# A delta-rule attention and two MoE layers on one core: the order of the first two solve groups rewritten

## The chip, the core and the metric

One core of a Trainium2 chip runs the whole program in one launch. Its engines are TensorE (PE, with its weight loads shown apart as PEld), VectorE (DVE), ScalarE (ACT), GpSimd (POOL) and SyncE (SP, which issues most DMAs). Each engine works through its own instructions in the order in which they were written and waits on semaphores for the others. The metric is device microseconds of one launch, as the median of several runs.

## The reference, cut to what matters

```python
def _attn_ref(q, k, v, beta):            # B=4, H=8, S=768, D=48
    k_n = k / (np.linalg.norm(k, axis=-1, keepdims=True) + 1e-06)
    for t in range(S):
        y[:, :, t] = np.einsum('bhd,bhde->bhe', q[:, :, t], state)
        v_old = np.einsum('bhde,bhd->bhe', state, kt)
        state = state + bt[:, :, :, None] * np.einsum('bhd,bhe->bhde', kt, vt - v_old)

def _moe_ref(x, w_gate, w1, w2):         # N=3072, 384 wide, 8 experts of 1024
    P = sinkhorn(exp(x @ w_gate - max))  # 8 rounds
    for e in range(E):
        out += P[:, e:e + 1] * (np.maximum(x @ w1[e], 0.0) @ w2[e])

def _moe2_ref(x, w_in, w_out):           # 384 -> 2048 -> 384
    h = x @ w_in
    return (h / (1 + exp(-1.702 * h))) @ w_out
```

The three run one after the other: the output of the attention, 3072 rows of 384, is the input of the first MoE layer, whose output is the input of the second. Only the attention has a step-by-step recurrence.

## The kernel before, in words

**Units and groups.** The 768 steps are cut into pieces of 64 tokens. Two batches are worked on at once, so there are 24 units (`NU`), numbered u. A unit's 64 steps are done together: a triangular system of 64 by 64 per head is solved ahead of time, and the state S goes from unit to unit only through four small matrix products. Four units make a group (`NG` = 6 groups, g), and the triangular solve is done for a whole group at once.

**The chain of a unit** (`chain`, L357 to L416) has four steps s. Step 0: `ks` on PE (keys times state, L373), then `r` on DVE (`ks` minus the values, L375), and two ACT copies of S into `su`. For the first unit there is no state, and `r` is the negated values, by ACT (L379). Step 1: `up` on PE (the inverse times `r`, L384) and two ACT copies into `su` (L385, L386). Step 2: `sp` on PE (L395) and the new S, by DVE (L401) or, for unit 0, ACT (L399). Step 3: `y` on PE (L408) and a copy `ys` by ACT (L410).

**The solve of a group** (`prep`, L209 to L355) is a generator. It makes norms, weights (`wt`), masks (`bm`, L168) and scores (`pg` on PE, L182), masks the scores into `am` (L188), copies two strips of `am` (L266), transposes them into `ln` (L269), and runs a loop of 30 dependent steps on DVE (jj, L275 to L299, two operations each, `lt` then `ln`) that inverts the 32 by 32 diagonal blocks. Then `ln` is transposed twice, into `ta` (L314) and `tt` (L340), and the off-diagonal quarter is filled by `pz` and `px` on PE (L323, L332), each with two ACT copies after it. `up` of a unit needs its 8 of the group's 32 blocks of `tt` finished.

**Two generators interleaved.** The main loop walks through units and steps, t = 4u + s. After each step of the chain, `slot(t)` advances `prep` by so many pieces as a table says (`FIRST[t]` for t up to 15, `PIECES` after that). A jj step is worth one piece. From t = 10 (`LAG`) on, slots also put in pieces of expert 0 of the first MoE layer: logits `pl`, then `ph` and `po` (matrix products in three passes, L499 to L501). So expert 0 can first run when units 0 and 1 are done and their output `xb` is split, and from there it fills PE. The work of engines is thus ordered at build time: this code decides only in which order each engine sees its instructions.

**Weights of expert 0.** `split0` advances a generator that writes the low parts of the weights (`w1s`, `w2s`, L545), four DVE subtractions at each of four calls. Before, two calls lie in the head of group 1 and two in its loop, at jj 4 and 10.

After the attention the kernel runs the remaining seven experts and the second layer, in which PE is filled. The change doesn't touch that part.

Of the kernel before, what the change touches and what calls it, by code (L numbers as in the profile page):

```python
# [9 lines left out]
F32 = mybir.dt.float32  # L10
# [11 lines left out]
H = 8  # L22
D = 48
# [5 lines left out]
PIECES = (4, 2, 2, 1, 2, 4, 4, 4, 4, 4, 4, 4, 3, 3, 2, 2)  # L29
ITEMS = (6, 5, 5, 5, 5, 5, 5, 5, 5, 5, 5, 6, 5, 5, 5, 5)  # L30

FIRST = (0, 4, 3, 2, 2, 2, 2, 3, 3, 4, 5, 5, 5, 4, 4, 4)


LAG = 10
# [5 lines left out]
class Attention:  # L41
# [167 lines left out]
    def prep(self, g):  # L209

        nc, am, tt = self.nc, self.am, self.tt
        w, u = 2 * g, 4 * g
        if g == 0:
            self.square(0, nc.vector)
            self.square(1, nc.vector)
            self.norm(0)
            self.norm(1)
            self.weigh(0, 1)
            self.mask(0, eng=nc.vector)
            for v in range(1, 4):  # L220
                self.mask(v)
            for v in range(4):
                self.gram(v, (0,), 0, H, (self.psc, "c") if v < 2 else None)
            self.scale_v(0)
            self.scale_k(0)
            self.square(2)
            self.square(3)
            self.at = {(0, 13): lambda: [self.gram(v, (1,), 0, H) for v in range(4, 8)],
                       (0, 20): lambda: self.kept.update({v: self.gram(v, (0,), 0, H, self.early[v - 4])
                                                          for v in range(4, 8)}),  # L230
                       (0, 23): lambda: self.split0(), (1, 4): lambda: self.split0(), (1, 10): lambda: self.split0()}
            yield 1.0
        elif g == 1:
            self.weigh(2, 3)
            nc.gpsimd.tensor_copy(out=self.gate, in_=self.w[3][:, 1, 7:8])
            self.scale_k(1)
            self.mask_m(2)
            self.mask_m(3)
            yield 1.0
            for v in range(4, 8):  # L240
                self.mask(v, eng=nc.vector)
                self.kept[v]()
                if v % 2:
                    self.split0()
                yield 1.0
        else:
            for i in range(8):
                if i == 5:
                    self.mask(u + 3)
                self.gram(u + i // 2, (0, 1), i % 2 * 4, 4)  # L250
                if i == 1:
                    self.square(w + 1)
                elif i == 2:
                    self.norm(w + 1)
                elif i == 3:
                    self.weigh(w + 1)
                    self.mask(u + 2)
                elif i == 7:
                    self.scale_k(w)
                    self.scale_k(w + 1)  # L260
                yield 1.0

        ln = self.one.tile([128, 32, 32], F32, tag="ln", name="ln")

        for q in (32, 96):
            (nc.vector.tensor_copy if g == 0 and q == 32 else nc.scalar.copy)(  # L266
                out=am[q:q + 32, :, 0:32], in_=am[q:q + 32, :, 32:64])
            yield 1.0
        nc.vector.transpose(out=ln, in_=am[:, :, 0:32].rearrange("p m t -> p t m"))  # L269
        if g == 0:  # L270
            for v in range(4):
                self.gram(v, (1,), 0, H)
        yield 1.0
        nc.vector.memset(ln.rearrange("p t s -> p (t s)")[:, 0:1024:33], 1.0)
        for jj in range(1, 31):  # L275
            tmp = self.one.tile([128, 256], F32, tag="lt", name="lt")
            nr = 31 - jj
            t3 = tmp[:, 0:nr * jj].rearrange("p (a c) -> p a c", c=jj)
            nc.vector.tensor_tensor(  # L279
                out=t3, in0=ln[:, jj + 1:32, jj:jj + 1].to_broadcast([128, nr, jj]),  # L280
                in1=ln[:, jj:jj + 1, 0:jj].to_broadcast([128, nr, jj]), op=ALU.mult)
            yield 0.5
            nc.vector.tensor_tensor(out=ln[:, jj + 1:32, 0:jj], in0=ln[:, jj + 1:32, 0:jj], in1=t3, op=ALU.add)  # L283
            if (g, jj) in self.at:
                self.at[g, jj]()
            if 0 < g < NG - 1:
                if jj == 17:
                    self.square(w + 2)
                elif jj == 21:
                    self.norm(w + 2)  # L290

            if jj == 22 and 0 < g < NG - 1:
                step = self.weights(w + 2)
            elif jj > 22 and 0 < g < NG - 1:
                next(step, None)
            if jj == 30 and 1 < g < NG - 1:
                self.mask(u + 4)
                self.mask(u + 5)
            yield 0.5  # L299
        if g < 2:  # L300
            nc.gpsimd.tensor_copy(out=self.gate, in_=ln[:, 31, 29:30])
            if g == 0:
                self.mask_m(0)
                self.mask_m(1)
            else:
                self.scale_k(2)
                for v in range(4, 8):
                    self.mask_m(v)
                    if v == 5:
                        self.scale_k(3)  # L310
                self.mask(8)
                self.mask(9)
        ta = self.one.tile([128, 32, 32], F32, tag="ta", name="ta")
        nc.vector.transpose(out=ta.rearrange("p m s -> p s m"), in_=ln.rearrange("p t s -> p s t"))  # L314
        yield 1.0

        zs = ta

        def pz(m0, n):
            ps = self.psg.tile([128, n, 32], F32, tag="g", name="pz")  # L320
            for m in range(n):
                for q in (0, 64):
                    nc.tensor.matmul(ps[q + 32:q + 64, m], am[q:q + 32, m0 + m, 32:64],  # L323
                                     ta[q:q + 32, m0 + m], start=True, stop=True, tile_position=(q, q + 32))
            for q in (0, 64):
                nc.scalar.copy(out=zs[q + 32:q + 64, m0:m0 + n], in_=ps[q + 32:q + 64])

        def px(m0, n):
            ps = self.psg.tile([128, n, 32], F32, tag="g", name="px")
            for m in range(n):  # L330
                for q in (0, 64):
                    nc.tensor.matmul(ps[q:q + 32, m], zs[q + 32:q + 64, m0 + m],  # L332
                                     tt[q + 32:q + 64, m0 + m, 32:64], start=True, stop=True,
                                     tile_position=(q + 32, q))
            for q in (0, 64):
                nc.scalar.copy(out=tt[q:q + 32, m0:m0 + n, 32:64], in_=ps[q:q + 32])

        def tr(q, m0=0, n=32):
            if q is None:
                nc.vector.transpose(out=tt[:, :, 32:64].rearrange("p m t -> p t m"), in_=ln)  # L340
            else:
                nc.scalar.copy(out=tt[q:q + 32, m0:m0 + n, 0:32], in_=tt[q:q + 32, m0:m0 + n, 32:64])

        for f, *i in (((pz, 0, 16), (tr, None), (pz, 16, 16), (tr, 0), (tr, 64), (px, 0, 16), (px, 16, 16)) if g else
                      ((pz, 0, 8), (tr, None), (tr, 0, 0, 8), (tr, 64, 0, 8), (px, 0, 8), (tr, 0, 8, 24),
                       (tr, 64, 8, 24), (pz, 8, 8), (px, 8, 8), (pz, 16, 16), (px, 16, 16))):
            while f == tr and self.upped < u - 1:
                yield 1.0
            f(*i)
            if f == px and i[0] == 0:  # L350
                self.ready = g
                if g == 0:
                    self.norm(2)
                    self.norm(3)
            yield 1.0  # L355

    def chain(self, u):  # L357

        nc = self.nc
# [3 lines left out]
        x, tt, bk = self.X[w % 4], self.tt, self.bk[w % 4]  # L363
        tk = [slice(64, 128), slice(0, 64)]
        S = self.S
        r = self.wk.tile([128, H, D], F32, tag="r", name="r", bufs=1)

        su = self.wk.tile([128, 2, H, D], F32, tag="su", name="su", bufs=1)
        if not first:
            ks = self.psc.tile([128, H, D], F32, tag="c", name="ks")  # L370
            for h in range(H):
                for b in range(2):
                    nc.tensor.matmul(ks[tk[b], h], x[64 * b:64 * b + D, 0, j, h], S[64 * b:64 * b + D, h],  # L373
                                     start=True, stop=True)
            nc.vector.tensor_tensor(out=r, in0=ks, in1=self.V[w][:, j], op=ALU.subtract)  # L375
            nc.scalar.copy(out=su[0:64, 0], in_=S[0:64])
            nc.scalar.copy(out=su[64:64 + D, 1], in_=S[64:64 + D])
        else:
            nc.scalar.mul(r, self.V[w][:, j], -1.0)  # L379
        yield  # L380
        up = self.psc.tile([128, H, D], F32, tag="c", name="up")
# [79 lines left out]
def kernel(  # L461
# [281 lines left out]
    def slot(t):  # L743

        n, k = rate * ITEMS[t % 16] if t >= LAG else 0, (PIECES if t > 15 else FIRST)[t % 16]
        if t == LAG:
# [447 lines left out]
```

## Time and profile before

| | |
|---|---|
| median of 3 runs | 2224.41 us (2222.56 to 2230.47) |
| the profiled execution | 2232.75 us, its span 2230.4 us |
| PE, DVE, ACT, POOL busy in the span | 97%, 68%, 48%, 49% |
| first `pl` of expert 0 | 89.43 us after the start |
| first `pz` of group 1 | 115.00 us |
| mean granted TensorE clock | 0.975 of full speed |

A row of the timeline gives the start in us, the length in us, the engine, line, operation and tiles; in square brackets the idle time of the engine just ahead of it and what ended that. A row with x2 or x4 covers so many instructions in a line, and its length runs from the start of the first to the end of the last. PEclk is the clock that was granted to TensorE, as a share of full speed.

### The profile page before, as it was taken

Reading aid. Unit: us, or ns where it says so; the run is one execution under the profiler, and the core shown is the slowest. Engines: PE = TensorE matmul, PEld = TensorE weight load, DVE = VectorE, ACT = ScalarE, POOL = GpSimd, SP = SyncE. Lnnn points to the kernel's source line nnn. Section 1 sums busy time; section 2 is a strip of 40 time slices with the busy share of each in tenths; the row PEclk is TensorE's granted clock in tenths of the full one; section 3 lists DMA queues with packets and bytes.
Section 4 is the critical chain, followed back from the end, with each engine's and each line's share of the span. In section 5 each row is a group of like instructions: output and inputs, shape, how many; then the busy total and the mean of one; then the engine's idle time right before and its main releaser. Section 6 shows DMA issues by size and latency. Waiting matters only on the chain.

```text
span 2230.4 us, 40903 instructions
## 1 busy us (share of the span) xinstructions
PE 2156.8 (97%) x15663; PEld 1953.7 (88%) x15663; DVE 1526.7 (68%) x2792; ACT 1068.0 (48%) x2126; POOL 1096.8 (49%) x1275
## 2 busy tenths in 40 slices
PE   5799999998999999999999999999999999999999
PEld 4778888896989999999999999999999989889998
DVE  7847775627777777767776777777775556776676
ACT  4334434434444544444445444455544446565554
POOL 4141123224776776666552656556665434662333
PEclk8689999998999999999999999999999999999999
DMA  6223333348335343333448655565554465567231
GB/s 159 51 62 81 105 100 102 90 127 294 136 115 184 124 168 136 115 144 110 159 164 275 185 178 182 170 200 178 188 199 143 136 239 164 172 192 246 92 121 50
DMA packets 229154, 336.74 MB, mean 151 GB/s; under 512 B 15648, under 2 KB 192416, under 8 KB 224800
## 3 DMA queue, kind: packets, MB, share of 16 engines
q1 hardware_dynamic: 228096, 332.86, 46.1%
q8 instruction: 123, 2.02, 0.4%
q10 hardware_dynamic: 864, 1.28, 0.2%
q14 instruction: 71, 0.58, 0.1%
HBM read 204.58 MB, written 129.50 MB: 150 GB/s over the span
## 4 chain that ended last, share of the span: by engine, by line
PE 85%; DVE 9%; DMA 2%; POOL 1%; ACT 1%; issue 1%; SPq 0%; POOLq 0%; ACTq 0%; DVEq 0%
PE po L501 14%; PE po L499 14%; PE po L500 14%; PE c L500 11%; PE c L501 11%; PE c L499 11%; DVE lt L279 3%; DVE ln L283 3%; PE ph L499 1%; PE pg L182 1%; PE ph L500 1%; PE ph L501 1%; PE y L408 1%; PE sp L395 1%; PE px L332 1%
## 5 line engine op out<-in xcount | busy, mean ns | idle before, releaser
L501 PE MATMUL po<-w2c,h 128*128 128x384 f32 x1728 | 586.6, 339 | 1.4 <-DVE h L1007 1.3
L500 PE MATMUL po<-w2c,h 128*128 128x384 f32 x1728 | 587.3, 340 | 0.0
L499 PE MATMUL po<-w2c,h 128*128 128x384 f32 x1728 | 578.5, 335 | 1.1 <-ACT h L1005 1.1
L1062 POOL TENSOR_TENSOR acc<-acc,ye 128x384 f32<-128x384 f32 x252 | 261.6, 1038 | 381.7 <-ACT ye L1061 329.6
L501 PE MATMUL c<-xt,w1c 128*128 128x512 f32 x1080 | 429.1, 397 | 2.0 <-POOL w1c L496 2.0
L499 PE MATMUL c<-xt,w1c 128*128 128x512 f32 x1080 | 424.5, 393 | 4.4 <-DVE f L1039 2.3
L500 PE MATMUL c<-xt,w1c 128*128 128x512 f32 x1080 | 428.0, 396 | 0.0
L1039 DVE TENSOR_TENSOR o<-o,c 128x512 f32<-128x512 f32 x288 | 197.5, 686 | 246.7 <-PE c L501 231.5
L1064 DVE SCALAR_TENSOR_TENSOR acc<-po,P,acc 128x384 f32<-128x384 f32 x420 | 258.2, 615 | 150.6 <-PE po L501 150.3
L499 PEld LDWEIGHTS po<-w2c,h 128*128 128x128 f32 x1728 | 324.9, 188 | 41.0 <-ACT h L1005 1.7
L500 PEld LDWEIGHTS po<-w2c,h 128*128 128x128 f32 x1728 | 323.8, 187 | 40.1
L501 PEld LDWEIGHTS po<-w2c,h 128*128 128x128 f32 x1728 | 325.0, 188 | 4.3 <-DVE h L1007 4.3
L1061 ACT ACTIVATE ye<-po,P 128x384 f32<-128x384 f32 x252 | 146.6, 582 | 372.1 <-PE po L501 359.3
L501 PEld LDWEIGHTS c<-xt,w1c 128*128 128x128 f32 x1080 | 202.3, 187 | 47.0 <-POOL w1c L496 2.8
L996 ACT ACTIVATE h<-f 128x512 fp32r<-128x512 f32 x224 | 133.9, 598 | 192.8 <-DVE f L1039 191.0
L499 PEld LDWEIGHTS c<-xt,w1c 128*128 128x128 f32 x1080 | 203.0, 188 | 18.8 <-DVE f L1039 3.1
L1039 DVE TENSOR_TENSOR f<-o,c 128x512 f32<-128x512 f32 x288 | 199.2, 692 | 20.7 <-PE c L501 3.6
L500 PEld LDWEIGHTS c<-xt,w1c 128*128 128x128 f32 x1080 | 203.0, 188 | 9.8
L1032 ACT COPY o<-c 128x512 f32<-128x512 f32 x288 | 163.6, 590 | 59.7 <-PE c L501 58.2
L496 POOL TENSOR_TENSOR w2c<-w2r,w2c 128x384 fp32r<-128x384 f32 x140 | 149.4, 1067 | 47.7 <-ACT w2c L495 47.4
L1074 POOL TENSOR_TENSOR acc<-acc,ye 128x384 f32<-128x384 f32 x84 | 92.7, 1104 | 156.6 <-ACT ye L1073 154.0
L998 DVE SCALAR_TENSOR_TENSOR h<-f,h 128x512 fp32r<-128x512 f32 x224 | 153.1, 683 | 21.2 <-ACT h L996 21.1
(177 smaller groups left out, 3410.2 us busy)
## 6 DMA issues: line engine op xcount, KB each, us to landing
w1c<-wd SPq DMA_DIRECT2D x210, 384.0 KB, 4.4
wd<-w1c SPq DMA_DIRECT2D x28, 1920.0 KB, 7.0
xs<-bo SPq DMA_DIRECT2D x184, 128.0 KB, 2.2
xt<-xs SPq DMA_DIRECT2D x46, 512.0 KB, 6.6
w2r<-in_w_dram SPq DMA_DIRECT2D x55, 384.0 KB, 6.0
wd<-wo SPq DMA_DIRECT2D x56, 256.0 KB, 2.9
w1r<-in_w_dram SPq DMA_DIRECT2D x28, 384.0 KB, 7.6
x<-in_kq_dram SPq DMA_DIRECT2D x24, 384.0 KB, 6.5
```

The source lines that it names most:

```text
L496: eng.tensor_tensor(out=dst_lo, in0=src, in1=dst_hi.bitcast(F32), op=ALU.subtract)
L499: nc.tensor.matmul(ps, lhs[0], rhs[0], start=start, stop=False, **kw)
L500: nc.tensor.matmul(ps, lhs[0], rhs[1], start=False, stop=False, **kw)
L501: nc.tensor.matmul(ps, lhs[1], rhs[0], start=False, stop=stop, **kw)
L996: nc.scalar.activation(out=h[:, 0], in_=src, func=ACTF.Relu)
L998: nc.vector.scalar_tensor_tensor(out=h[:, 1], in0=src, scalar=0.0, in1=h[:, 0].bitcast(F32), op0=ALU.max, op1=ALU.subtract)
L1032: nc.scalar.copy(out=o, in_=ps)
L1039: nc.vector.tensor_tensor(out=d, in0=o, in1=ps, op=ALU.add if how == "add" else ALU.subtract)
L1061: nc.scalar.mul(ye, ps, P[:, u, e:e + 1])
L1062: nc.gpsimd.tensor_tensor(out=a, in0=a, in1=ye, op=ALU.add)
L1064: nc.vector.scalar_tensor_tensor(out=a, in0=ps, scalar=P[:, u, e:e + 1], in1=a, op0=ALU.mult, op1=ALU.add)
L1074: nc.gpsimd.tensor_tensor(out=a, in0=a, in1=ye, op=ALU.add)
```

## The change

It does five things. (1) `r` of unit 0 is made in the head of group 0, ahead of the loop, and no longer in the chain. (2) The norms, weights, masks and masked scores of group 1, which stood at the start of that group's own generator, move into the tail of group 0, right behind its first `px`; on POOL the masking of `x` comes ahead of the scaling of the keys. (3) The tail of group 0 is reordered: both remaining `pz` come right behind that, the remaining two `px` after them. (4) Both strip copies of group 1 go to DVE. (5) The four `split0` calls move to group 1's strip copy and to jj 6, 11 and 16 of its loop, and `FIRST` changes from 52 pieces in all to 50. Every later group then stands about one piece earlier against the chain, as the last of the orders below shows.

```diff
-FIRST = (0, 4, 3, 2, 2, 2, 2, 3, 3, 4, 5, 5, 5, 4, 4, 4)
+FIRST = (0, 2, 3, 2, 3, 3, 3, 3, 3, 4, 4, 4, 4, 4, 4, 4)
...
             self.scale_v(0)
+            self.r = self.wk.tile([128, H, D], F32, tag="r", name="r", bufs=1)
+            nc.scalar.mul(self.r, self.V[0][:, 0], -1.0)
             self.scale_k(0)
...
-                       (0, 23): lambda: self.split0(), (1, 4): lambda: self.split0(), (1, 10): lambda: self.split0()}
+                       (0, 23): lambda: self.split0()}
+            for jj in (6, 11, 16):
+                self.at[1, jj] = lambda: self.split0()
             yield 1.0
-        elif g == 1:
-            self.weigh(2, 3)
-            nc.gpsimd.tensor_copy(out=self.gate, in_=self.w[3][:, 1, 7:8])
-            self.scale_k(1)
-            self.mask_m(2)
-            self.mask_m(3)
-            yield 1.0
-            for v in range(4, 8):
-                self.mask(v, eng=nc.vector)
-                self.kept[v]()
-                if v % 2:
-                    self.split0()
-                yield 1.0
-        else:
+        elif g > 1:
...
-            (nc.vector.tensor_copy if g == 0 and q == 32 else nc.scalar.copy)(
+            (nc.vector.tensor_copy if g == 1 or (g, q) == (0, 32) else nc.scalar.copy)(
                 out=am[q:q + 32, :, 0:32], in_=am[q:q + 32, :, 32:64])
+            if (g, q) == (1, 96):
+                self.split0()
...
+        def second():
+            self.norm(2)
+            self.norm(3)
+            self.weigh(2, 3)
+            nc.gpsimd.tensor_copy(out=self.gate, in_=self.w[3][:, 1, 7:8])
+            self.mask_m(2)
+            self.mask_m(3)
+            self.scale_k(1)
+            self.mask(4, eng=nc.vector)
+            self.kept[4]()
+            self.mask(5, eng=nc.vector)
+
+        def take(*vs):
+            for v in vs:
+                if v > 5:
+                    self.mask(v, eng=nc.vector)
+                self.kept[v]()
...
-                      ((pz, 0, 8), (tr, None), (tr, 0, 0, 8), (tr, 64, 0, 8), (px, 0, 8), (tr, 0, 8, 24),
-                       (tr, 64, 8, 24), (pz, 8, 8), (px, 8, 8), (pz, 16, 16), (px, 16, 16))):
+                      ((pz, 0, 8), (tr, None), (tr, 0, 0, 8), (tr, 64, 0, 8), (px, 0, 8), (second,),
+                       (pz, 8, 8), (pz, 16, 16), (take, 5, 6), (tr, 0, 8, 24), (tr, 64, 8, 24), (px, 8, 8),
+                       (take, 7), (px, 16, 16))):
```

**On PE, at the end of group 0** (the solve's `pz` and `px`, the chain's `up` and `sp` of unit 0), before:

```order
L323 MATMUL pz<-ta,am 32x32 x16
L332 MATMUL px<-tt,ta 32x32 x16
L384 MATMUL up<-r,tt 64x48 x16
L323 MATMUL pz<-ta,am 32x32 x16
L332 MATMUL px<-tt,ta 32x32 x16
L395 MATMUL sp<-su,bk_147 64x48
```

And now, at the same place:

```order
L316 MATMUL pz<-ta,am 32x32 x16
L325 MATMUL px<-tt,ta 32x32 x16
L393 MATMUL up<-r,tt 64x48 x16
L316 MATMUL pz<-ta,am 32x32 x48
L404 MATMUL sp<-su,bk_147 64x48
```

The two remaining `pz` now stand together ahead of `sp`, and the second `px`, which waited for a copy of `pz` by ACT, no longer stands ahead of `sp`. Further on, behind that `sp`, PE now has:

```order
L417 MATMUL y<-su,x_125 64x48 x16
L325 MATMUL px<-tt,ta 32x32 x16
L382 MATMUL ks<-S,x_125 64x48 x16
L325 MATMUL px<-tt,ta 32x32 x32
L393 MATMUL up<-r,tt 64x48 x16
```

The two `px` lie on either side of `ks` of unit 1 and ahead of its `up`.

**On DVE, from `r` of unit 1 to the transpose that starts group 1's loop**, before:

```order
L375 TENSOR_TENSOR r<-ks,v 128x384
L168 TENSOR_TENSOR bm<-nmask,wt 128x512
L188 TENSOR_TENSOR am<-pg,bm 128x512
L168 TENSOR_TENSOR bm<-nmask,wt 128x512
L188 TENSOR_TENSOR am<-pg,bm 128x512
L545 TENSOR_TENSOR w1s_191<-wr,w1s_191 128x384
L545 TENSOR_TENSOR w1s_192<-wr,w1s_192 128x384
L545 TENSOR_TENSOR w2s_199<-wr,w2s_199 128x384
L545 TENSOR_TENSOR w2s_200<-wr,w2s_200 128x384
L496 TENSOR_TENSOR xb<-xt,xb 128x3x128
L401 TENSOR_TENSOR S<-S,sp 112x384
L269 STREAM_TRANSPOSE ln<-am 128x1024
```

And now:

```order
L384 TENSOR_TENSOR r<-ks,v 128x384
L257 COPY am<-am 32x32x32 x2
L554 TENSOR_TENSOR wgs<-wgr,wgs 128x3x8
L554 TENSOR_TENSOR w1s_189<-wr,w1s_189 128x384
L554 TENSOR_TENSOR w1s_190<-wr,w1s_190 128x384
L554 TENSOR_TENSOR w2s_197<-wr,w2s_197 128x384
L554 TENSOR_TENSOR w2s_198<-wr,w2s_198 128x384
L505 TENSOR_TENSOR xb<-xt,xb 128x3x128
L262 STREAM_TRANSPOSE ln<-am 128x1024
```

All four pairs of `bm` and `am` now lie ahead of `r`, the strip copies are DVE's own, and S of unit 1 comes behind the second step of the loop.

**On PE, at the end of group 2**, where the solve's `pz` meets unit 7's `up` and the turning of the output of unit 6 (`xt`), before:

```order
L499 MATMUL ph<-xb,w1s_193 128x256
L500 MATMUL ph<-xb,w1s_193 128x256
L501 MATMUL ph<-xb,w1s_193 128x256
L384 MATMUL up<-r,tt 64x48 x16
L499 MATMUL ph<-xb,w1s_193 128x256
L500 MATMUL ph<-xb,w1s_193 128x256
L501 MATMUL ph<-xb,w1s_193 128x256
L421 MATMUL xt<-ident,ys 128x128 x3
L323 MATMUL pz<-ta,am 32x32 x32
```

And now:

```order
L316 MATMUL pz<-ta,am 32x32 x32
L508 MATMUL ph<-xb,w1s_193 128x256
L509 MATMUL ph<-xb,w1s_193 128x256
L510 MATMUL ph<-xb,w1s_193 128x256
L393 MATMUL up<-r,tt 64x48 x16
L508 MATMUL ph<-xb,w1s_193 128x256
L509 MATMUL ph<-xb,w1s_193 128x256
L510 MATMUL ph<-xb,w1s_193 128x256
L430 MATMUL xt<-ident,ys 128x128 x3
```

The first `pz` of the group has moved ahead of `up` and `xt`; groups 3, 4 and 5 show the same.

## Rows read from the trace of the kernel before

**Rows 1.** The page, parts 1 and 2: engines, and granted clock in 40 slices.

```profile
PE 2156.8 (97%) x15663; PEld 1953.7 (88%) x15663; DVE 1526.7 (68%) x2792; ACT 1068.0 (48%) x2126; POOL 1096.8 (49%) x1275
...
PEclk8689999998999999999999999999999999999999
```

**Rows 2.** Windows of 20 us: length, busy of PE, PEld, DVE, ACT, POOL, PEclk, DMA share, GB/s.

```profile
60.00:80.00 20.00, 16.22 (x331) 14.88 (x327) 12.68 (x20) 9.68 (x17) 3.44 (x3) 0.50 0.20 49
80.00:100.00 20.00, 15.23 (x157) 13.69 (x158) 17.05 (x44) 4.18 (x10) 1.49 (x1) 0.67 0.37 93
100.00:120.00 20.00, 16.06 (x284) 14.35 (x284) 16.43 (x46) 6.40 (x14) 7.22 (x7) 0.85 0.11 31
120.00:140.00 20.00, 17.84 (x319) 15.01 (x318) 9.08 (x25) 9.05 (x17) 11.62 (x10) 0.90 0.28 62
140.00:160.00 20.00, 20.00 (x217) 16.67 (x216) 7.62 (x19) 4.86 (x11) 5.58 (x5) 0.74 0.23 70
180.00:200.00 20.00, 19.13 (x333) 17.27 (x332) 16.44 (x47) 7.04 (x17) 3.48 (x3) 0.91 0.27 82
```

**Rows 3.** Timeline, the chain of units 0 and 1.

```profile
51.62 0.51 ACT L379 ACTIVATE r<-v 128x384 f32<-128x384 f32 x1
52.18 1.94 PE L384 MATMUL up<-r,tt 64*64 64x48 f32 x32 [1.65 <-ACT r L379]
...
68.81 0.56 DVE L375 TENSOR_TENSOR r<-ks,v 128x384 f32<-128x384 f32 x1 [4.88 <-PE ks L373]
...
69.52 1.95 PE L384 MATMUL up<-r,tt 64*64 64x48 f32 x32 [0.82 <-DVE r L375]
```

**Rows 4.** Waits from 45 to 96 us: total, times, longest, in us.

```profile
PE px L332 <- ACT ta L326: 3.0, 3, 2.0
```

**Rows 5.** Timeline, DVE and POOL: strip copies, masks, weight splits, start of a loop.

```profile
20.10 1.19 DVE L266 COPY am<-am 32x1024 f32<-32x1024 f32 x1
...
54.94 1.30 DVE L168 TENSOR_TENSOR bm<-nmask,wt 128x512 f32<-128x512 f32 x1
55.78 6.30 POOL L207 TENSOR_TENSOR x<-x,bm 64x512 f32<-64x512 f32 x4
59.35 4.59 DVE L545 TENSOR_TENSOR w2s<-wr,w2s 128x384 fp32r<-128x384 f32 x2
...
71.94 1.02 DVE L545 TENSOR_TENSOR w1s<-wr,w1s 128x384 fp32r<-128x384 f32 x2
...
73.81 0.55 DVE L496 TENSOR_TENSOR xb<-xt,xb 128x384 fp32r<-128x384 f32 x1
...
77.03 1.94 DVE L269 STREAM_TRANSPOSE ln<-am 128x1024 f32<-128x1024 f32 x1 [2.16 <-ACT am L266]
...
79.04 0.17 DVE L279 TENSOR_TENSOR lt<-ln 128x30 f32<-128x30 f32 x1
```

**Rows 6.** Timeline, from expert 0's first matmul to the end of group 1.

```profile
89.43 0.38 PE L499 MATMUL pl<-xb,wgs 128*8 128x256 f32 x1
...
105.87 1.14 PE L384 MATMUL up<-r,tt 64*64 64x48 f32 x32 [2.11 <-DVE r L375]
...
112.88 2.06 DVE L314 STREAM_TRANSPOSE ta<-ln 128x1024 f32<-128x1024 f32 x1
115.00 1.20 PE L323 MATMUL pz<-ta,am 32*32 32x32 f32 x64 [1.83 <-DVE ta L314]
```

**Rows 7.** Timeline, the end of group 2 and the start of group 3's loop.

```profile
191.62 1.13 PE L384 MATMUL up<-r,tt 64*64 64x48 f32 x32
...
193.15 0.49 PE L421 MATMUL xt<-ident,ys 128*128 128x128 f32 x3
...
194.51 1.20 PE L323 MATMUL pz<-ta,am 32*32 32x32 f32 x64 [0.87 <-DVE ta L314]
...
236.93 0.42 DVE L654 SCALAR_TENSOR_TENSOR h<-ph,h 128x256 fp32r<-128x256 f32 x1 [1.37 <-ACT h L653]
```

**Rows 8.** PE's waits from 90 to 600 us: total, times, longest, in us.

```profile
PE pz L323 <- DVE ta L314: 4.8, 5, 1.8
```

More of the change, by code (lines that the diff above doesn't have):

```diff
@@ L349, in prep @@
             f(*i)
-            if f == px and i[0] == 0:
+            if f in (px, second) and (g > 0 or f == second) and i[0:1] in ([0], []):
                 self.ready = g
-                if g == 0:
-                    self.norm(2)
-                    self.norm(3)
             yield 1.0
@@ L365, in chain @@
         S = self.S
-        r = self.wk.tile([128, H, D], F32, tag="r", name="r", bufs=1)
+        r = self.wk.tile([128, H, D], F32, tag="r", name="r", bufs=1) if u else self.r
         su = self.wk.tile([128, 2, H, D], F32, tag="su", name="su", bufs=1)
@@ L377, in chain @@
             nc.scalar.copy(out=su[64:64 + D, 1], in_=S[64:64 + D])
-        else:
+        elif u:
             nc.scalar.mul(r, self.V[w][:, j], -1.0)
```

## Prediction

> **What bounds the kernel now.** I read the page first. PE is busy for 97% of the span, and the granted clock is low only in the first slices [rows 1]. So the change can win in two ways only: PE's full stretch begins earlier, or PE stalls less within it. Each microsecond that expert 0 begins earlier is one off the end, because the same matmuls follow in nearly the same number; each microsecond for which PE then waits is one back.
>
> Next the windows show how the start looks [rows 2]. From 60 to 80 us PE has work for 16 of 20 us, but at 0.50 of full speed, and DVE for 13. From 80 us on DVE is the full one (17 of 20), and PE reaches full work and clock in steps. So up to 89.43 us, where expert 0's first matmul stands [rows 6], the kernel is a relay between PE, ACT and DVE, and after that PE is fed while DVE runs group 1's loop. The reader should see two waits there: PE waits 2.11 us for r of unit 3 and 1.83 us for `ta` [rows 6]; both are DVE's. So up to 115 us group 1's loop on DVE sets the pace, and what counts is how early that loop starts and how much foreign work lies in it.
>
> **The change, part by part. r of unit 0.** PE's `up` of unit 0 waited 1.65 us, at the end of it for ACT's r of 0.51 us [rows 3]. Made before the loop, r lies in a stretch in which ACT has nothing else to do for 10 us or so, and costs nothing; if that cover were gone it would cost its 0.51. What ends the wait now is the copy of `px`, right ahead of r. Gain 0.5 us.
>
> **pz together, px later.** Between the starts of the two `up` rows lie 17.34 us [rows 3]. In them PE waited 3.0 us in `px` for ACT's copies of `pz` [rows 4] and 0.82 us for r [rows 3]. In the new order other matmuls fill those waits: `pz`, `sp` and `y` lie between, and the two ACT copies of each `pz` have ended when `px` comes. All 3.8 us can go, but the last part of 0.82 only if r hides behind the last `px`, which stands between `ks` and `up`. So `up` of unit 1 starts at 69.52 - 0.5 - 3.8 = 65.2 us. It can't be less than nothing gained here, and not more than 4.3.
>
> **DVE's way to the loop.** r of unit 1 then starts some 2 us earlier than that `up` (one `px` of 64, 1.20 us at full clock [rows 6], times 1.94/1.13 for the half clock [rows 3, 7]), at 63.3, and ends at 63.9. Behind it lie two strip copies of 1.19, one tiny subtraction (0.2, like the smallest loop step), four weight splits of 0.51, `xb` of 0.55 and the transpose, 1.94 [rows 5]: 7.1 us, so the loop starts at 71.0 and not at 79.04, 8.0 us earlier. Gone are the two mask pairs behind r and the 2.16 us for which DVE waited for ACT's strip copies [rows 5].
>
> **In the loop.** There are three blocks of weight splits now, and there were two: 4 x 0.51 = 2.04 us more on DVE [rows 5]. S of unit 1 comes in and S of unit 3 goes behind `ta`, which cancels. So `ta` gains 6.0.
>
> **The masks beside POOL.** The last three mask products now run straight behind the first, while POOL masks `x` in four pieces (6.30 us [rows 5]) and then scales keys and values. DVE's operations with both inputs in SBUF are slowed beside POOL: two splits of 0.51 took 4.59 us, and a mask 1.30 [rows 5]. The price here lies between nothing (DVE has some 2 us of slack ahead of r) and 4.59 - 1.02 = 3.6 us. I take 1.0: three masks are slowed as in the 1.30 row or more, and the slack takes most. The Trainium skill (SBUF — State Buffer, "Who interferes with whom") has it that a DVE instruction with two SBUF inputs contends with a GpSimd instruction that reads SBUF, and that the loser fully blocks. The 4.59 us agree. By that rule the last mask, which needs the fourth piece, could block behind both scalings that follow on POOL, and the price would be nearer the upper end.
>
> So `ta` comes 6.0 - 1.0 = 5.0 us earlier. PE's own way there (r of unit 3 is behind three split blocks and two more loop steps) gains some 0.5 less, which the vanishing 1.83 us wait doesn't quite cover. The first `pz` of group 1 gains **4.5 us**.
>
> **Later groups.** Their order on PE has changed: the first `pz` of groups 2 to 5 stands ahead of `up` and `xt`. In group 2 that work ran from 191.62 to 193.64 us, while DVE made `ta`, and PE then waited 0.87 us more [rows 7]; over five groups these waits are 4.8 us [rows 8]. If DVE's loop doesn't start earlier against PE, the wait grows by those 2.0 us in each of four groups, 8.0 in all. But the strip copies are ahead by a piece as well. In group 3 DVE waited 1.37 us in an `h` ahead of the transpose [rows 7]; that `h` comes behind it now, which gives most of the 2.0 back. I have this row for one group, and elsewhere about half. So the cost lies between 0 and 8.0, and I take 2.5 in all.
>
> **Sum.** -4.5 + 2.5 = -2.0 us. Against the profiled execution's own 2232.75 us this gives 2230.7. That run is 8.3 us above the median of 2224.41, so for the median I take the same difference: **2222 us**, 0.1% faster. A measurement of this kernel tells about 0.5%, 11 us, from no change.
>
> **The rivals.** (a) *The stalls of later groups win, slower.* `pz` waits for `ta` at 2.0 us more in each group: -4.5 + 8.0 = +3.5, 2228 us. And a stall can draw more: behind the 0.87 us wait at 194 the clock fell, and the window shows 0.91, 1.8 us lost [rows 2]. If three more groups draw that, 5.4 us come on top, 2233 us. It decides from 1.1 us a group on (4.5 / 4). For it: DVE is the full engine in these loops. Against it: the earlier transposes.
>
> (b) *The clock does better.* From 100 to 160 us the granted clock is 0.85, 0.90 and 0.74 [rows 2]: between full speed and these lie 20 x (0.15 + 0.10 + 0.26) = 10.2 us of PE's time, in three falls, each a few microseconds behind a stall. The `ta` stall of 1.83 us goes nearly away, so a fall may, but the stall for r of unit 3 may grow. If all went, 2222 - 10 = 2212 us.
>
> (c) *The clock rises early.* In the new order PE runs from 51.7 to about 72 us nearly without a gap. The clock was 0.50 all through 60 to 80 us, though PE was busy for 81% of it [rows 2], so I hold it at half. If it rose at some 57 us, `up`, `sp`, `y` and `ks` would take 1.14 and not 1.95 [rows 3, 6]. DVE would then hold the relay, so that of some six such steps only two, 1.6 us, count, and the first 4 us of expert 0 at half clock (89.43 to about 93, in the window of 0.67 [rows 2, 6]) would save 2 more: 3.6 us in all, 2218 us. The Trainium skill (TensorE: Matmul & The Clock Gate, "What's actually happening") says that the default is throttled and activity releases it. That rule speaks for (c); the trace of this stretch, with small tiles, so far speaks against it.
>
> (d) *The early gain isn't there.* POOL blocks the masks at the full 3.6 us: 2.6 us less gain, 2225 us, no change.
>
> **How the numbers follow.** I give the forecast 0.50 (alone, 2218 to 2227), (a) 0.18, (b) 0.13, (c) 0.09 and (d) 0.10. The range reaches to (b) with one us and to (a) with its clock falls nearly: 2211 to 2232, which leaves some 0.15 out. Faster by over 0.5%, that is under 2213.3, needs (b) nearly in full or with (c): 0.11. Slower by over 0.5% needs (a) with long falls of the clock behind each stall, over 2235.5: 0.07. The rest, 0.82, is within.
>
> **What would show it.** Right: `up` of unit 1 at 65 to 66 us; the first step of group 1's loop at 71 to 72; expert 0's first matmul at 85 to 86; group 1's first `pz` at 110 to 111; PE's waits for `ta` in groups 2 to 5 at 5 to 6 us in total (they are 4.8 - 1.83 = 3.0 now [rows 6, 8]). Wrong: masks of 2 us and more ahead of r of unit 1; a granted clock above 0.5 before 80 us; stalls of 2 us and more ahead of `pz` in each later group; or a shift at 120 us that isn't found again at 500, where the attention is over.

## The result, and the profile after

The changed kernel takes **2249.08 us** (median of 4 runs, 2247.34 to 2254.19). The kernel before, on the same chip, takes 2223.48 us (4 runs, 2219.58 to 2230.47). The ratio is 1.0114, with a 95% interval of 1.0094 to 1.0134: the change costs 25.6 us. The forecast was 2222 us, and its range ended at 2232.

The profiled execution of after took 2247.34 us, with a span of 2245.0 us. Parts 1 and 2 of its page, against [rows 1]:

```profile
PE 2160.0 (96%) x15663; PEld 1956.3 (87%) x15663; DVE 1522.2 (68%) x2794; ACT 1065.3 (47%) x2124; POOL 1097.3 (49%) x1275
...
PEclk7789998999999999999999999999999999999999
```

PE has the same 15663 matmuls and 3 us more of busy time; the engines' totals tell nothing of 25 us. Of the granted clock four digits differ, the first and second (7 and 7, were 8 and 6), the seventh (8, was 9; 337 to 393 us) and the tenth (9, was 8). The seventh lies where the change was expected to do little. So the next view is the timeline, first at the start, then at the ends of later groups:

```profile
50.95 1.94 PE L393 MATMUL up<-r,tt 64*64 64x48 f32 x32 [0.89 <-ACT tt L329]
...
59.99 1.47 POOL L162 TENSOR_TENSOR bk<-bk,wt 128x768 f32<-128x768 f32 x1
60.06 3.38 DVE L168 TENSOR_TENSOR bm<-nmask,wt 128x512 f32<-128x512 f32 x1 [1.71 <-POOL x L207]
61.42 1.47 POOL L113 TENSOR_TENSOR v<-v,nn 128x768 f32<-128x768 f32 x1
...
64.84 1.95 PE L393 MATMUL up<-r,tt 64*64 64x48 f32 x32 [1.34 <-ACT tt L329]
...
71.30 0.17 DVE L272 TENSOR_TENSOR lt<-ln 128x30 f32<-128x30 f32 x1
...
84.82 0.38 PE L508 MATMUL pl<-xb,wgs 128*8 128x256 f32 x1
...
105.44 2.07 DVE L307 STREAM_TRANSPOSE ta<-ln 128x1024 f32<-128x1024 f32 x1
107.57 1.20 PE L316 MATMUL pz<-ta,am 32*32 32x32 f32 x64 [1.64 <-DVE ta L307]
...
264.31 2.05 DVE L307 STREAM_TRANSPOSE ta<-ln 128x1024 f32<-128x1024 f32 x1
...
266.42 1.66 PE L316 MATMUL pz<-ta,am 32*32 32x32 f32 x64 [2.46 <-DVE ta L307]
...
269.27 0.99 PE L393 MATMUL up<-r,tt 64*64 64x48 f32 x14
...
495.53 0.67 PE L393 MATMUL up<-r,tt 64*64 64x48 f32 x16
```

The start won what it should, and more. Against [rows 3, 5, 6], `up` of unit 1 is 4.7 us earlier, group 1's loop 7.7 (71.30, was 79.04), expert 0's first matmul 4.6, group 1's first `pz` 7.4. Then the lead melts. The transposes into `ta` of groups 1 to 5 stand at 105.44, 186.88, 264.31, 345.18 and 429.56 us; before they stood at 112.88, 192.21, 267.54, 341.65 and 416.67. That is -7.4, -5.3, -3.2, +3.5, +12.9: some 2 us are lost in the first groups and 7 to 9 in each of the last two steps. The last `up` (495.53) is 13.7 us late.

What is lost there the timeline shows at 264 to 269 us. `ta` starts right behind its loop, and PE, which has `pz` next in its row, stands still for 2.46 us while DVE transposes. In [rows 7], at the end of group 2 of the kernel before, `up` and `xt` fill PE's time during that transpose; here `up` comes at 269.27, behind `pz`. PE's waits from 95 to 500 us, total, times and longest, after:

```profile
PE pz L316 <- DVE ta L307: 10.8, 5, 2.5
PE up L393 <- DVE r L384: 8.1, 4, 2.4
PE pg L182 <- DVE x L201: 4.6, 3, 2.3
```

and in the kernel before, beside [rows 8] (there `pg` waits for `x` only once, for ACT):

```profile
PE up L384 <- DVE r L375: 6.6, 4, 2.3
...
PE pg L182 <- ACT x L550: 0.6, 1, 0.6
```

At `pz` the waits are 6.0 us longer, at `pg` and `up` together 5.5. Windows of after (span and length, PE busy, PEclk, DMA share, GB/s) show what comes behind two of these waits, the 2.46 us that end at 266.42 and the 2.12 us that end at 347.28:

```profile
260.00:264.00 4.00, 3.95 (x52) 1.00 0.04 11
264.00:268.00 4.00, 1.58 (x64) 0.85 0.00 0
268.00:272.00 4.00, 4.00 (x42) 0.50 0.02 4
272.00:276.00 4.00, 4.00 (x81) 0.79 0.01 2
276.00:280.00 4.00, 4.00 (x106) 1.00 0.56 150
...
344.00:348.00 4.00, 1.88 (x52) 1.00 0.00 0
348.00:352.00 4.00, 4.00 (x71) 0.59 0.02 4
352.00:356.00 4.00, 4.00 (x73) 0.50 0.15 42
356.00:360.00 4.00, 4.00 (x44) 0.63 0.62 175
360.00:364.00 4.00, 4.00 (x107) 1.00 0.52 152
```

PE is busy all the time behind the wait, but at 1.2 GHz for part of the next 12 us. Against full speed that is 4 x (0.50 + 0.21) = 2.8 us lost behind the first (and 0.6 in the window of the wait), 4 x (0.41 + 0.50 + 0.37) = 5.1 us behind the second. The wait is paid, and then paid again.

### The profile page after: what moved, and what is told of

It reads as the page before. It is cut to its first block, busy times and chain, and to the rows that moved or that the text cites. A ratio compares the mean times of both kernels' runs of the same rounds, so it can differ in the third digit from the quotient of the medians.

```text
span 2245.0 us, 40894 instructions
## 1 busy us (share of the span) xinstructions
PE 2160.0 (96%) x15663; PEld 1956.3 (87%) x15663; DVE 1522.2 (68%) x2794; ACT 1065.3 (47%) x2124; POOL 1097.3 (49%) x1275
## 4 chain that ended last, share of the span: by engine, by line
PE 82%; DVE 10%; POOL 3%; DMA 2%; issue 2%; ACT 1%; SPq 0%; POOLq 0%; ACTq 0%; DVEq 0%
PE po L510 14%; PE po L508 14%; PE po L509 14%; PE c L509 10%; PE c L510 10%; PE c L508 10%; DVE ln L276 2%; DVE lt L272 2%; PE ph L508 1%; PE pg L182 1%; POOL w1c L505 1%; DMA w1r<-in_w_dram 1%; PE ph L509 1%; PE ph L510 1%; PE up L393 1%
## 5 line engine op out<-in xcount | busy, mean ns | idle before, releaser
L508 PEld LDWEIGHTS c<-xt,w1c 128*128 128x128 f32 x1080 | 203.2, 188 | 18.6 <-DVE f L1048 3.7
```

Of the source, the lines that this page charges most:

```text
L508: nc.tensor.matmul(ps, lhs[0], rhs[0], start=start, stop=False, **kw)
```

## The experiments

**Theory.** The cost is in the later groups: their first `pz` waits for `ta`, because `up` and `xt` no longer stand ahead of it, and each long wait draws a fall of the clock. **Rivals:** the early part does harm that shows late; or the whole order of later groups, a piece ahead, makes r, h and x late, and `pz` only adds its wait; or the order is innocent and the clock fell by chance.

The first four runs separate the early stage from the later order. e1 is the changed kernel with the last entry of the table lowered by one, so that from group 2 on every engine's order is that of before:

```
-FIRST = (0, 2, 3, 2, 3, 3, 3, 3, 3, 4, 4, 4, 4, 4, 4, 4)
+FIRST = (0, 2, 3, 2, 3, 3, 3, 3, 3, 4, 4, 4, 4, 4, 4, 3)
```

> The changed kernel with the last entry of FIRST at 3 and not 4, so that from group 2 on every engine has its instructions in the order of the kernel before; groups 0 and 1 stay as changed. Theory 1 (the later groups standing one piece ahead costs, the early part gains): the loop of group 1 starts at 71 to 72 us, group 5's ta comes at 408 to 412 us (before 416.67, after 429.56), ratio to before 0.995 to 0.999. Theory 2 (the early part itself costs later, by the clock or by contention, and the later order is neutral): ratio stays at 1.007 or more.

e2 is the kernel before with the same shift the other way, so that the later groups run in the order of after:

```
-FIRST = (0, 4, 3, 2, 2, 2, 2, 3, 3, 4, 5, 5, 5, 4, 4, 4)
+FIRST = (0, 4, 3, 2, 2, 2, 2, 3, 3, 4, 5, 5, 5, 4, 4, 5)
```

> The kernel before with the last entry of FIRST at 5 and not 4: the order of groups 0 and 1 stays as before, and from group 2 on every engine has the order of the changed kernel. Theory 1: ratio 1.012 to 1.018, above that of the whole change since its early gain is missing; PE's waits for ta in groups 2 to 5 rise from 3.0 to about 9 us. Theory 2: ratio 0.997 to 1.003.

e3 is the changed kernel with one piece put between `ta` and the first `pz` of groups 2 to 5, and one taken out behind it:

```
+            if g > 1 and f == pz and i[0] == 0:
+                yield 1.0
             f(*i)
 ...
-            yield 1.0
+            if not (g > 1 and f == pz and i[0] == 0):
+                yield 1.0
```

> The changed kernel with the first pz of groups 2 to 5 one piece later, behind up and xt as in the kernel before, all else as changed. If the place of pz alone is what costs (theory 1a): the waits for ta fall from 9 to 3 or 4 us, and the time falls by 6 to 12 us, ratio to before 1.005 to 1.008. If it is the whole order standing ahead (theory 1b): the waits for ta fall, but those for r, x and h stay or grow, and the ratio stays within 1.009 to 1.013.

e4 is the kernel before once more, for its profile.

> The kernel before once more, for a second profile. Every theory: 2219 to 2231 us, group 5's ta within 5 us of 416.67; stalls of PE at the same places, falls of the clock behind them in part at other places.

The next four ask whether that one place is all. e5 is the kernel before with only the first `pz` of groups 2 to 5 a piece earlier (no yield between `ta` and it, one behind it). e6 is e1 with the edit of e3. e8 is e1's edit once more, to 2. e7 asks what the early stage is worth, by a delay of known size in e1:

```
+        if g == 1:
+            for _ in range(3):
+                nc.vector.transpose(out=ln, in_=am[:, :, 0:32].rearrange("p m t -> p t m"))
         nc.vector.transpose(out=ln, in_=am[:, :, 0:32].rearrange("p m t -> p t m"))
```

> The kernel before, with one thing alone changed: the first pz of groups 2 to 5 stands in PE's row ahead of up and xt (one ph or po piece, up, one piece and xt now follow it), as in the changed kernel; all other matmuls keep their places. Theory 1 (the place of that pz is the cost: PE stands 2 us at it in every group, and the clock falls behind it): PE's waits on ta 9 to 11 us in groups 1 to 5 (4.8 before), and 2236 to 2244 us, ratio 1.006 to 1.010, since moving it back gained 19 us from the changed kernel. Rival (the cost is the whole strip standing a piece ahead, with r, h and x late, and the pz only adds its own wait): waits on ta the same 9 to 11, but 2225 to 2231 us, ratio 1.001 to 1.004.

> The changed kernel with the later groups put back in step with the order of before, and the first pz of groups 2 to 5 one ph or po piece further behind xt than before had it. Theory 1 (waits on ta cost themselves and the clock): waits on ta fall from 3.5 to under 1.5 us in all, and the time from 2222.7 to 2214 to 2220, ratio 0.996 to 0.999. Rival (before's place is already late enough, what is left of the wait is covered or moves to px): 2221 to 2225, ratio 0.999 to 1.001.

> The realigned kernel with the transpose of am into ln ahead of the loop of group 1 done four times instead of once: VectorE spends 5.8 us more there (1.94 us each), with the same values and the same order of everything else. Theory A (a microsecond of the early stage counts in full at the end): the first unit of group 1 and all behind it 5 to 6 us later, ratio 1.0013 to 1.0027 (0.9992 plus 0.0026). Theory B (the early stage has slack against what comes behind: weight loads, the clock, later waits): the delay fades, as the early gain did from 4 us at unit 4 to 2 at unit 5, and the ratio stays at 0.998 to 1.0005.

> The changed kernel with the last number of the first table at 2 instead of 4: the later groups' preparation stands a piece further behind the units than in the kernel before, where the change had put it a piece ahead. Theory 1 (only how long PE stands at pz and pg for what it is put ahead of): waits on ta under 1.5 us in all, and 2214 to 2222 us, ratio 0.996 to 1.000. Rival (any step away from the order of before costs some 7 us, as the rest did when the pz alone was put back): 2226 to 2232 us, ratio 1.001 to 1.004.

The last four measure the price of a wait without moving anything, and finish two pairs. e9 is the kernel before with the edit of e3, e10 is e6 with the delay of e7. e11 and e12 are the kernel before with part or all of one transpose done twice (`0:16` in e11, `0:32` in e12):

```
+        if g > 1:
+            nc.vector.transpose(out=ta.rearrange("p m s -> p s m")[:, 0:16], in_=ln.rearrange("p t s -> p s t")[:, 0:16])
         nc.vector.transpose(out=ta.rearrange("p m s -> p s m"), in_=ln.rearrange("p t s -> p s t"))
```

> The kernel before, with the first pz of groups 2 to 5 one ph or po piece further behind xt, and nothing else moved. Putting it so in the realigned kernel brought its ratio from 0.9992 to 0.9967. Theory 1 (that gain is pz's own, whatever the early stage does): 0.9965 to 0.9985, 2216 to 2220 us. Rival (the gain of that kernel is the early stage's, which the realigned kernel lost to the clock by chance): 0.999 to 1.001.

> The realigned kernel with pz later, with 5.8 us of VectorE's time (three more transposes of am into ln, the same values) ahead of the loop of group 1. Theory A (the early stage counts in full): ratio 0.9985 to 1.0000 (0.9967 plus 0.0026). Theory B (the early stage is mostly covered by what follows it): 0.996 to 0.9975.

> The kernel before, in its own order, with ta late by 1.0 us in groups 2 to 5: half of its transpose is done twice (the same values). PE's wait at the first pz rises by 1.0 us in each, to 1.9, 1.3, 1.6 and 2.3. Theory 1 (a wait of PE there costs itself, and where it is long the clock as well): 4 us from the waits, and 0 to 6 from the clock: 2227 to 2234 us, ratio 1.002 to 1.005. Rival (the waits alone): 2227.5, 1.0018. Rival (covered by the work behind): 0.999 to 1.001.

> The kernel before, in its own order, with the whole transpose into ta done twice in groups 2 to 5, 2.0 us later in each; the first pz waits 2.9, 2.3, 2.6 and 3.3 us, about as in the kernel that has only the pz ahead (2.96, 3.18, 2.86, 3.34, and 27 us slower). Theory 1 (the length of the wait is what costs, by itself and by the clock behind it, no matter what stands where): 2239 to 2252 us, ratio 1.007 to 1.013, with a granted clock of 0.5 to 0.9 in the 12 us behind most of these waits. Rival (what costs there is the order, the up and xt that stand behind the waiting pz, and a wait costs its length): 2231 to 2234, ratio 1.003 to 1.005.

**What was measured.** The columns: median (of 4 to 12 runs, e4 of one); ratio with its 95% interval, each against runs of before on the same chip (their medians 2223.08 to 2223.62); and from each profiled execution PE's waits on `ta` and all PE waits with a named releaser from 95 to 500 us, and the clock's loss, the sum over the 20 windows from 100 to 500 us of 20 x (1 - PEclk). All in us.

| kernel | median | ratio | on `ta` | all waits | clock |
|---|---|---|---|---|---|
| before; e4 | 2223.48; 2221.9 | 1 | 4.8; 4.0 | 16.6; 17.0 | 17.2; 11.6 |
| after | 2249.08 | 1.0114 (1.0094 to 1.0134) | 10.8 | 29.0 | 24.2 |
| e1 after, realigned | 2222.74 | 0.9992 (0.9975 to 1.0009) | 3.5 | 19.2 | 17.2 |
| e2 before, later order of after | 2253.73 | 1.0127 (1.0111 to 1.0144) | 12.5 | 29.9 | 25.8 |
| e3 after, `pz` later | 2230.01 | 1.0033 (1.0012 to 1.0053) | 1.1 | 23.1 | 27.6 |
| e5 before, `pz` ahead | 2250.36 | 1.0126 (1.0106 to 1.0146) | 15.7 | 26.7 | 37.8 |
| e6 e1, `pz` later | 2217.22 | 0.9967 (0.9953 to 0.9981) | 3.2 | 19.4 | 8.8 |
| e7 e1, early delay | 2223.85 | 0.9998 (0.9984 to 1.0012) | 5.1 | 18.8 | 8.4 |
| e8 e1, a piece further behind | 2252.74 | 1.0118 (1.0099 to 1.0137) | 13.6 | 31.0 | 30.6 |
| e9 before, `pz` later | 2222.1 | 0.9996 (0.9986 to 1.0005) | 3.1 | 15.6 | 17.2 |
| e10 e6, early delay | 2220.25 | 0.9988 (0.9975 to 1.0001) | 2.5 | 16.3 | 12.0 |
| e11 before, `ta` 1.2 later | 2232.22 | 1.0050 (1.0032 to 1.0069) | 11.0 | 23.0 | 19.0 |
| e12 before, `ta` 2.2 later | 2244.61 | 1.0094 (1.0080 to 1.0108) | 15.2 | 27.7 | 25.4 |

The profiled executions of e3 (span 2240.3) and e5 (span 2258.8) are among the longest of their kernels, that of e6 (2209.8) is the shortest, and that of before took 2232.75 us, 9 us above its median, so their last columns lie off the median too. In e6 2.3 of the 19.4 us of waits belong already to what follows the attention.

**The early part is innocent, the later order is all of it.** e1 has the whole early part and costs nothing that can be told from zero; e2 has none of it and costs 1.27%. Theory 1 had both sides right. But it gave e1 0.995 to 0.999 with group 5's `ta` at 408 to 412 us; `ta` came at 414.31, so of the 5.0 us by which e1 leads before at group 1's `ta` (107.92) some 2.4 were left by then. Theory 2, which put the harm in the early part, falls.

**One matmul burst's place is enough.** In e5 only the four `pz` have moved, and the ratio is 1.0126, as with the whole later order. I had expected 1.006 to 1.010, with waits on `ta` of 9 to 11 us; they are 15.7, 12.3 of it at the four `pz` that were moved. Timeline of e5, end of group 3, and windows of 4 us there:

```profile
271.32 2.04 DVE L314 STREAM_TRANSPOSE ta<-ln 128x1024 f32<-128x1024 f32 x1
273.42 1.92 PE L324 MATMUL pz<-ta,am 32*32 32x32 f32 x64 [3.18 <-DVE ta L314]
...
276.20 1.95 PE L387 MATMUL up<-r,tt 64*64 64x48 f32 x32
```

```profile
268.00:272.00 4.00, 2.23 (x37) 1.00 0.00 0
272.00:276.00 4.00, 2.58 (x67) 0.66 0.00 0
276.00:280.00 4.00, 4.00 (x41) 0.50 0.02 4
280.00:284.00 4.00, 4.00 (x84) 0.98 0.29 58
```

`pz` has waited 3.18 us, longer than the transpose; then its own 64 small matmuls take 1.92 us and not 1.20, and `up` 1.95 and not 1.13, at half clock.

**It is not about being ahead.** e8 was expected to be safe: its `pz` stands behind `xt` in PE's row, and my theory gave 0.996 to 1.000. It is 1.0118. The timeline of its group 3 shows why:

```profile
271.21 0.56 DVE L505 TENSOR_TENSOR xb<-xt,xb 128x384 fp32r<-128x384 f32 x1 [1.71 <-ACT xb L504]
271.69 2.03 DVE L307 STREAM_TRANSPOSE ta<-ln 128x1024 f32<-128x1024 f32 x1
...
273.86 1.70 PE L316 MATMUL pz<-ta,am 32*32 32x32 f32 x64 [2.84 <-DVE ta L307]
```

Now DVE has `xb` ahead of `ta` in its own row, and `xb` waits for PE's `xt` and ACT's cast. So `ta` starts 1.71 us late, and PE, with one piece of work behind `xt`, stands for 2.84 us. One step forward PE comes too early, one step back DVE comes too late. In groups 2 and 5 it is an `h` ahead of `xb` that waits (1.13 and 1.04 us), with the same end: `pz` waits 2.94 and 2.96 us. My expectation looked at PE's row alone; the rival, "any step away from the order of before costs some 7 us", had the side right, and the price at about a quarter.

**The price of a wait, by itself.** e12 changes no engine's order. Its second transpose starts 2.09 to 2.21 us behind the first, 8.6 us in four groups, and costs 20.9 us (0.0094 x 2223). In e11 it is 1.18 to 1.24 us, 4.9 in all, and costs 11.1. That is 2.4 and 2.3 us for each microsecond. (The intervals of the two ratios allow 2.1 to 2.8, and 1.5 to 3.1.) PE's waits on `ta` in e12 and, around the start of its first late `pz` at 195.81, behind a wait of 2.91 us, windows of 4 us:

```profile
PE pz L325 <- DVE ta L316: 15.2, 5, 3.8
```

```profile
191.81:195.81 4.00, 1.09 (x15) 1.00 0.01 2
195.81:199.81 4.00, 4.00 (x106) 0.69 0.21 54
199.81:203.81 4.00, 4.00 (x72) 0.50 0.00 1
203.81:207.81 4.00, 4.00 (x21) 0.53 0.34 98
207.81:211.81 4.00, 4.00 (x127) 1.00 0.51 110
```

The loss is 4 x (0.31 + 0.50 + 0.47) = 5.1 us, more than the wait. Behind the other three it is 4.9, 1.7 and 5.1 us in the 12 us that follow. In the table the waits on `ta` rise by 10.4 us from before to e12 (1.5 of it in group 1, where nothing was changed) and the clock's loss by 8.2 (13.8 against e4), 18.6 to 24.2 in all, and 20.9 were measured. So in e12 nothing else is needed; the rival that gave 1.003 to 1.005 falls, and so does e11's "waits alone" (1.0018, where the interval begins at 1.0032). The length of the waits isn't quite all, though: the four waits of e5 add up to 12.3 us and those of e12 to 11.8, and yet e5 costs 28.0 us and e12 20.9. Whether those 7 us are the price of `up` and `xt` behind a waiting `pz`, or chance (the intervals just touch), no run tells.

**What e3 left.** With `pz` put back, PE's waits on `ta` in groups 2 to 5 are gone, and the changed kernel is still 0.33% slower than before: less than either expectation gave (1.005 to 1.008 if the place of `pz` alone costs, 1.009 to 1.013 if the whole order does). Its waits from 95 to 500 us:

```profile
PE up L396 <- DVE r L387: 8.6, 4, 2.7
PE pg L182 <- DVE x L201: 5.3, 4, 2.3
...
PE pz L316 <- DVE ta L307: 1.1, 1, 1.1
```

The waits at `pg` and `up` are those of after; they came with the shifted order too. One more of that order lies behind 500 us, outside the table. In after it ends at 520.65 us; from PE's waits from 500 to 560 us:

```profile
PE ph L508 <- DVE h L663: 2.9, 1, 2.9
```

This wait is 2.9 us in e2 and 2.6 in e3 as well, and none of the other eleven profiles has one of over 1 us there. That these waits make the rest of some 7 us is argued from the rows; no run took them away alone. The parts don't add up (28.0 for `pz` alone in e5, 7.3 without it in e3, 25.6 in after): in e5 the four waits last 2.86 to 3.34 us, in after 2.12 to 2.46.

**What the early gain is worth.** Three pairs differ in the early part alone: before and e1, -0.0008; e2 and after, -0.0013; e9 and e6, -0.0029. That is 1.8, 2.9 and 6.4 us. Two pairs differ by the 5.8 us of delay: e1 and e7, +0.0006; e6 and e10, +0.0021, 1.3 and 4.7 us. All have the sign of theory A (it counts at the end), but e7's ratio lies in the range of theory B (0.998 to 1.0005) and e10's in that of A (0.9985 to 1.0000). Single intervals are about 0.0015 to either side, and e9 against e6 is the only pair whose intervals part. So the early part seems to bring 2 to 6 us, and how much of its lead (5 to 7 us at group 1's `ta`) survives stays open.

**A version that is faster than both.** e6, with the early part and the `pz` a piece further behind, takes 0.33% less than before (0.19 to 0.47%). Its waits on `ta` are 3.2 us, not the 1.5 expected, but 1.5 of them lie in group 1, whose `pz` this edit leaves in place. The place of `pz` alone isn't what won: in e9 it gives nothing (0.9996), against theory 1 there.

## Why the prediction was wrong, point by point

**The early stage was right, and better than the sum.** Foreseen were `up` of unit 1 at 65.2 (64.84), the loop at 71.0 (71.30), `pl` at 85 to 86 (84.82). The first `pz` gained 7.4 and not 4.5. The term "2.04 us more in the loop" was too large: from the loop's first step to `ta` it took 33.84 us before [rows 5, 6] and 34.14 after, since DVE waited less in it (before, 1.54 us for `xb` alone). That the loop's start came out so well is partly luck: r of unit 1, worked out without the masks for 63.3, started at 64.15, right behind the last mask product, and the two strip copies took 1.39 us together and not 2.38. So the masks did cost r some 0.85 of the 1.0 us, but nothing at `up`: what ended its wait was ACT's copy of `px` (row at 64.84), not r. The fourth mask took 3.38 us, beside POOL's two scalings of 1.47; the other three took 0.69, 1.23 and 0.69. The Trainium skill (SBUF — State Buffer, "Who interferes with whom") calls the port pair that DVE shares with GpSimd an exclusive lock; the fourth mask, which ended 0.55 us behind the second scaling, agrees. Rival (d) had its mechanism and not its price.

**Rival (c) fell.** From 60 to 72 us PE was busy for 10.1 of 12 us and from 50 to 60 for 9.1 of 10, and the granted clock was 0.50 throughout. The Trainium skill (TensorE: Matmul & The Clock Gate, "What's actually happening") has it that activity releases the throttle; these 22 us of small matmuls did not release it.

**The step that failed** is in "Later groups": "that `h` comes behind it now, which gives most of the 2.0 back", and so "the cost lies between 0 and 8.0, and I take 2.5 in all". The bound itself was good for the waits on `ta`: in groups 2 to 5 they rose from 3.0 to 9.1 us, 6.1 of the 8.0. So 1.9 us came back and not 5.5. The reason is in DVE's rows from r of unit 9 on, at the start of group 3's loop. Before:

```profile
235.00 0.56 DVE L375 TENSOR_TENSOR r<-ks,v 128x384 f32<-128x384 f32 x1 [1.22 <-PE ks L373]
...
239.77 0.56 DVE L496 TENSOR_TENSOR xb<-xt,xb 128x384 fp32r<-128x384 f32 x1 [0.53 <-ACT xb L495]
240.28 0.17 DVE L279 TENSOR_TENSOR lt<-ln 128x30 f32<-128x30 f32 x1
...
240.74 0.22 DVE L279 TENSOR_TENSOR lt<-ln 128x58 f32<-128x58 f32 x1
```

After:

```profile
231.57 0.56 DVE L384 TENSOR_TENSOR r<-ks,v 128x384 f32<-128x384 f32 x1 [1.57 <-PE ks L382]
...
234.30 0.17 DVE L272 TENSOR_TENSOR lt<-ln 128x30 f32<-128x30 f32 x1
...
236.32 0.56 DVE L505 TENSOR_TENSOR xb<-xt,xb 128x384 fp32r<-128x384 f32 x1 [1.61 <-ACT xb L504]
236.80 0.21 DVE L272 TENSOR_TENSOR lt<-ln 128x58 f32<-128x58 f32 x1
```

The `h` does come behind the transpose, and the loop's first step stands 2.73 us behind r and not 5.28. But `xb`, which stood ahead of the loop, now stands inside it and waits there for ACT: the second step is 5.23 us behind r, and was 5.74. In groups 2, 4 and 5 `xb` waits in the loop too, for 1.76, 1.36 and 1.47 us. The wait that was to vanish came back one step later, and the prediction had read one row of one group [rows 7]. This is read from the rows; no run moved `xb` alone.

**Two terms weren't in the sum at all.** The first is the price of a wait: 8.0 was taken as the far end, with 5.4 for the clock in rival (a) from one fall of 1.8 us [rows 2]. That fall stood behind a wait of 0.87 us; behind waits of 2 to 3 us in these kernels the windows show losses from nothing to 5.1 us, and e11 and e12 have the measured price, 2.3 to 2.4 us for one us. With it, 6.1 us of waits cost some 15. The second is the other waits that the shift made, 5.5 us at `pg` and `up` and 2.9 in the late `ph`; the prediction spoke of no wait of the later groups but the one at `ta`. Rival (a) named the right place with the right sign, at a chance of 0.18, and its 2228 to 2233 us were too low by these two. The prediction's own signs of being wrong came true: stalls of 2.15, 2.46, 2.12 and 2.41 us ahead of `pz` in the later groups, and a lead that was gone before 500 us. So did its mask of 2 us and more, the 3.38 above, but without harm at `up`.

**The balance.** From before to after: -7.4 at `ta` of group 1, +12.4 for all waits (29.0 - 16.6), +7.0 for the clock, in all +12.0; the last `up` is 13.7 us late. Against e4 the same sum is 12.0 + 12.6 - 6.7 = +17.9, and the last `up` of e4 (477.45 us) is 18.1 us earlier than in after. What is left up to 25 us lies behind that: from the last `up` to the end of the span after takes 1749.5 us, e4 1742.1, and before's own profile 1748.6. Up to 2.9 us of it can be the late wait in `ph`. For the rest no cause is shown: e4 and before are the same program and differ by 6.5 us there.

## What to carry to other kernels

In a queue that runs in order, an instruction that waits is placed by two rows at once: what its engine has to do ahead of it, and what the engine that it waits for has to do ahead of the result. Here one matmul burst a piece ahead cost 1.26% (e5) and a piece later nothing (e9), but the whole generator a piece later cost 1.18% (e8), because then another operation of DVE came ahead of the awaited result. So a table that shifts a whole generator by one is checked at every crossing of the two rows, and not only where the change is meant to act. A wait of PE is priced with the half-clock stretch behind it, and that price can be measured by making the awaited result late by a known amount.

## What the runs showed of the hardware

A wait of 2.91 us was followed by some 10 us of low granted clock (0.69, 0.50, 0.53 in windows of 4 us), though PE worked without a gap again; one of 2.15 us in after, which ended at 188.99, was followed by windows at 1.00. The same program lost 17.2 us to the clock in one profile and 11.6 in another. So a stall's price is a mean: the four waits of e12 cost 20.9 us together, but behind them the clock lost 5.1, 4.9, 1.7 and 5.1 us.
